# Output row stores released from one another in an attention, Fourier-mix and MLP kernel

## The chip, the cores and the metric

One core of a Trainium2 chip. The metric is device microseconds of one execution. Kernels that share a ratio were run in turn on the same chip; the experiments were timed in three calls (chips 0, 15 and 5), each with its own runs of the kernel before, so across calls compare ratios and not times. All runs quoted are in the fast state (none over 1.5% above the fastest of its kernel; two slower runs of the kernel before, at 295.54 and 295.11 us, are left out), except two single looks whose state is unknown (said where they stand). Ratios are the mean time of one kernel's runs over that of the other's of the same rounds, so not quite the ratio of the medians quoted beside them.

## The reference, cut to what matters

```python
def reference(q, k, v, sort_net, moe_w_ch1, moe_w_ch2):
    # attention over 4 batches, 8 heads, 768 tokens, head_dim 64,
    # keys and values mixed by blocks with a normalised sort_net
    x = attn_out.transpose(0, 2, 1, 3).reshape(4, 768, 512)
    mixed = real(fft(fft(x, axis=1), axis=2))
    u  = x + mixed
    un = layernorm(u)                      # no scale, no shift
    return u + maximum(un @ w_ch1, 0) @ w_ch2     # 512 -> 2048 -> 512
```

The output is 4 x 768 rows of 512 float32. The kernel computes it in 24 tiles of 128 rows: per batch a half g = 0 (tiles T = 0, 1, 2) and a half g = 1 (T = 3, 4, 5). It uses a symmetry of the Fourier transform, and the tiles of the second half therefore hold their tokens in descending order.

## The kernel before

The engines go by the profile's names: PE is TensorE (matmuls; PEld its weight loads), DVE VectorE, ACT ScalarE, POOL GpSimd, SP SyncE; a q after a name, as in POOLq, is that engine's sequencer. A store is a DMA, and it *lands* when its completion semaphore says so. A planner in the kernel records operations, puts them in an order per engine and issues them. What the change touches is the end of the MLP of one half (cuts marked):

```python
TOK = [list(range(1, 129)), list(range(129, 257)),
       list(range(257, 384)) + [0], list(range(767, 639, -1)),
       list(range(639, 511, -1)), list(range(511, 383, -1))]
# ...
many("u", 6, [128, DM], F32)            # six buffers for output tiles
# ...
for tt in range(3):
    # ... 16 matmuls of w_ch2 into bank ps ("ff2") ...
    V.tensor_tensor(u.ap, ps.ap, u.ap, op=ALU.add)          # residual add
    if T < 2:
        nc.sync.dma_start(out[b, t0:t0 + 128, :], u.ap)     # SP, plain
    elif T == 2:
        # ... three plain SP stores of 112, 15 and 1 rows ...
    else:
        i = 3 * b + T - 3
        nc.gpsimd.indirect_dma_start(                       # POOL, by row list
            out.rearrange("b s m -> (b s) m"),
            bass.IndirectOffsetOnAxis(ap=rows[:, i:i + 1], axis=0),
            u.ap, None)
```

Ascending rows go out as plain stores from SP. Descending rows go out as indirect stores from POOL, one row number per partition. The dependency tracker cannot see which rows an indirect store writes. It takes the whole output as written, and so it makes each indirect store wait for the landing of the one before, and plain and indirect stores wait for one another.

The softmax here doesn't subtract the row's maximum and nothing guards it: scores larger than these inputs give would overflow.

## Time and profile before

| | before |
|---|---|
| time, median of 4 runs | 292.62 us (291.86 to 292.87) |
| span of the profiled run (291.84 us, not one of the four) | 290.0 us |
| PE / DVE / ACT / POOL busy | 90% / 59% / 54% / 23% of the span |
| end of the last residual add | 281.57 + 0.69 = 282.26 us |
| from there to the end of the span, "the tail" | 7.74 us |

The first 110 us (loads, attention of the first batches) have idle PE; from 110 to 277 us PE is full; the tail is stores alone. The prediction shows these lines. Two more lines: what closes the span. The view is of the closing instructions of the program (count, then min/median/max in ns, first and last start in us).

```profile
L1377 SPq EVENT_SEMAPHORE  x11: 17/28/28, 288.1 to 290.0; - x11
...
L1377 POOLq DRAIN  x3: 46/97/4127, 285.1 to 289.8; - x3
```

SP gets past its wait for the last store at 288.1 us, which is its landing. POOL's closing DRAIN starts about 285.13 us, takes 4.127 us and ends at 289.26. The span ends 0.74 us later.

### The profile page before, as it was taken

How to read it: one execution, taken by the hardware profiler on the slowest of the kernel's cores; microseconds unless marked ns; L12 is line 12 of the kernel's file. 1: busy time of each engine (PE TensorE's matmuls, PEld its weight loads, DVE VectorE, ACT ScalarE, POOL GpSimd, SP SyncE). 2: the span in 40 equal slices, each digit the busy share in tenths (PEclk: the TensorE clock that was granted, in tenths of full speed). 3: DMA queues.
4: the chain of work that ended last, by engine and by line, in shares of the span. 5: the costliest groups of instructions: out<-in, count | busy, mean ns of one | idle time of the engine just before them, and what ended most of it. 6: DMA issues, size and time to landing. Idle time of an engine off the chain costs nothing.

```text
span 290.0 us, 5807 instructions
## 1 busy us (share of the span) xinstructions
PE 260.9 (90%) x2284; PEld 155.2 (54%) x2284; DVE 171.9 (59%) x405; ACT 157.9 (54%) x323; POOL 66.3 (23%) x104
## 2 busy tenths in 40 slices
PE   0389988897999999999999999999999999999980
PEld 0258866554565656554566456455555546545530
DVE  4697999999999999831579643145034226210020
ACT  2677979785778945970477037137415505425300
POOL 8973300015900640011220002032000212200021
PEclk9997999998899999999999999999999999999997
DMA  7999999910990897211113010311311111221001
GB/s 114 211 260 245 215 208 211 219 37 5 157 146 10 95 165 133 66 37 20 77 47 57 36 52 22 58 72 50 57 72 37 38 54 72 38 90 36 2 36 72
DMA packets 42529, 26.33 MB, mean 91 GB/s; under 512 B 30106, under 2 KB 38824, under 8 KB 42500
## 3 DMA queue, kind: packets, MB, share of 16 engines
q0 software_dynamic: 23536, 18.31, 37.4%
q1 hardware_dynamic: 18966, 7.64, 11.6%
q8 instruction: 18, 0.29, 0.4%
q14 instruction: 9, 0.07, 0.1%
HBM read 28.96 MB, written 6.29 MB: 122 GB/s over the span
## 4 chain that ended last, share of the span: by engine, by line
PE 62%; DVE 22%; DMA 8%; issue 3%; POOL 2%; ACT 1%; POOLq 0%; DVEq 0%
PE bank L1253 26%; PE bank L1274 25%; DMA hr<-in_v_dram 4%; DVE vsf L660 3%; DVE vcx L708 3%; DVE rt L1006 3%; DMA out_dram<-u,rows 2%; POOL kq L472 2%; DMA kq<-in_q_dram 2%; PE bank L1149 2%; PE bank L991 2%; DVE st L1186 1%; PE bank L952 1%; PE bank L897 1%; DVE ks L660 1%
## 5 line engine op out<-in xcount | busy, mean ns | idle before, releaser
L1265 ACT ACTIVATE hr<-bank 128x384 f16<-128x384 f32 x115 | 56.3, 491 | 75.2 <-PE bank L1253 74.4
L1253 PE MATMUL bank<-ut,w1sb 128*128 128x384 f16 x512 | 92.8, 329 | 0.7 <-ACT ut L660 0.7
L1274 PE MATMUL bank<-w2sb,hr 128*128 128x512 f16 x384 | 87.9, 379 | 0.0
L1253 PEld LDWEIGHTS <-w1sb 128*128 128x128 f16 x512 | 49.0, 99 | 34.8 <-issue 1.8
L1274 PEld LDWEIGHTS <-hr 128*128 128x128 f16 x384 | 36.7, 98 | 41.8 <-issue 0.2
L1282 DVE TENSOR_TENSOR u<-bank,u 128x512 f32<-128x512 f32 x24 | 16.5, 689 | 60.2 <-PE bank L1274 59.8
L961 ACT ACTIVATE ex<-bank 96x384 f32<-96x384 f32 x64 | 27.9, 485 | 6.3 <-PE bank L952 6.0
L1295 POOL DMA_INDIRECT out_dram<-u,rows x12 | 12.2, 1013 | 77.0 <-DVE u L1282 56.7
L1193 POOL TENSOR_SCALAR mv<-mv 128x3 f32<-128x3 f32 x8 | 1.9, 240 | 109.8 <-DVE mv L1188 109.8
L976 ACT ACTIVATE eb<-ex,negone 96x384 f16<-96x384 f32 x35 | 20.8, 615 | 0.2
L1213 ACT ACTIVATE un<-u,nm,ny 128x512 f16<-128x512 f32 x15 | 12.2, 810 | 11.8 <-DMA ut<-un 8.5
L1172 DVE SCALAR_TENSOR_TENSOR u<-rt,bank 128x510 f32<-128x510 f16 x12 | 8.1, 678 | 16.3 <-PE bank L1138 8.9
L991 PE MATMUL bank<-vsf,eb 97*128 97x65 f16 x416 | 16.5, 193 | 1.3 <-DVE rr L836 0.5
L1006 DVE TENSOR_TENSOR rt<-bank,rz 128x384 f16<-128x384 f32 x32 | 17.2, 549 | 0.3
L991 PEld LDWEIGHTS <-eb 97*128 97x128 f16 x416 | 15.4, 98 | 3.6 <-issue 1.3
L472 POOL DMA_DIRECT2D kq<-in_q_dram x20 | 16.4, 850 | 1.7 <-DMA kq<-in_q_dram 1.2
L1186 DVE BATCH_NORM_STATS2 st<-u 128x6 f32<-128x512 f32 x24 | 16.1, 686 | 0.3
L1160 DVE SCALAR_TENSOR_TENSOR u<-rt,bank 128x512 f32<-128x512 f16 x12 | 8.0, 684 | 13.9 <-PE bank L1153 13.5
L927 PE MATMUL bank<-pack,qr 128*128 128x128 f16 x48 | 4.8, 246 | 12.3 <-ACT qr L660 11.7
L724 PE MATMUL bank<-bdv,vcx 128*128 128x128 f16 (+1 forms) x128 | 12.6, 225 | 0.0
L952 PE MATMUL bank<-qt,ks 64*128 64x96 f16 x256 | 11.3, 207 | 1.3 <-DVE rt L1006 0.4
L897 PE MATMUL bank<-bdk,kq 128*64 128x128 f16 x192 | 10.7, 228 | 1.6 <-DVE bdk L636 0.8
(130 smaller groups left out, 338.2 us busy)
## 6 DMA issues: line engine op xcount, KB each, us to landing
kq<-in_k_dram POOLq DMA_DIRECT2D x8, 384.0 KB, 6.6
w1sb<-in_moe_w_ch_dram POOLq DMA_DIRECT2D x4, 512.0 KB, 16.0
w2sb<-in_moe_w_ch_dram POOLq DMA_DIRECT2D x4, 512.0 KB, 19.0
out_dram<-u SPq DMA_DIRECT2D x8, 256.0 KB, 2.0
kq<-in_q_dram POOLq DMA_DIRECT2D x4, 384.0 KB, 11.6
hr<-in_v_dram POOLq DMA_DIRECT2D x2, 768.0 KB, 11.2
kq<-in_v_dram POOLq DMA_DIRECT2D x2, 768.0 KB, 21.5
kq<-in_q_dram POOLq DMA_DIRECT2D x16, 96.0 KB, 5.5
```

Source lines behind the costliest of these rows:

```text
L472: o = P.add({eng: c}, lambda _: e.dma_start(dst, src), r=r, w=w, prio=prio, nbytes=nbytes, tag="load", after=after)
L897: nc.tensor.matmul(ps.ap[64 * h2:64 * h2 + 64, 128 * r3:128 * r3 + 128], k16[:, 2 * hl + h2, 3 * half + r3, :], bdk[:, 2 * hp + h2].rearra ...
L952: nc.tensor.matmul(pss[h2].ap[:, BLK * j:BLK * j + BLK], ks.ap[rows, 4 * g + j, :], qt.ap[rows, c0:c0 + BLK])
L961: nc.scalar.activation(ex.ap, pss[h2].ap[0:96, 0:384], AF.Exp, scale=SCALE),
L976: nc.scalar.activation(ed, src, AF.Identity, bias=negone[0:96])
L991: nc.tensor.matmul(po.ap[:, 65 * T:65 * T + 65], eb.ap[:, e0:e0 + 128], vsf[:, vi:vi + 65], start=(n == 0), stop=(n == len(WIN[T]) - 1), s ...
L1006: P.add({"DVE": (0.45, 0.56)}, lambda _: V.tensor_tensor(rt.ap[:, :, D * h:D * h + D], po3()[:, :, 0:D], rz.ap[:, :, None].broadcast_to([1 ...
L1186: P.add({"DVE": (0.6, 0.69)}, lambda _, u=u, st=st: V.bn_stats(st.ap, u.ap), r=[u], w=[st], tag="bn")
L1253: nc.tensor.matmul(ps.ap[:, 0:GT], w1sb[:, c, 128 * fc:128 * fc + 128], ut.ap[:, c, :], start=(c == 0), stop=(c == 3))
L1265: nc.scalar.activation(hr[g][:, fc, :], ps.ap[:, 0:GT], AF.Relu)
L1274: nc.tensor.matmul(ps.ap, hr[g][:, fc, 128 * tt:128 * tt + 128], w2sb[:, fc, :], start=(fc == 0), stop=(fc == 15))
L1282: V.tensor_tensor(u.ap, ps.ap, u.ap, op=ALU.add),
```

## The change

Each output row is stored exactly once, so no store has to wait for another. The change declares that to the dependency tracker. It puts a one-column memset ahead of each indirect store: without it the tracker refuses the release for two DMAs that are neighbours in one engine's issue order.

```diff
+    between = ct("between", [128, 1], F32)
...
                 else:
                     i = 3 * b + T - 3
-                    nc.gpsimd.indirect_dma_start(
+                    nc.gpsimd.memset(between, 0.0)
+                    st_ = [nc.gpsimd.indirect_dma_start(
                         ...
-                                                  axis=0), u.ap, None)
+                                                  axis=0), u.ap, None)]
+                for x in st_:
+                    for y in stores if T < 3 else stores + direct:
+                        tc.declare_no_dep(x.ins, y.ins,
+                                          reason="each row stored once")
+                (stores if T > 2 else direct).extend(st_)
```

(The plain stores are put in a list `st_` likewise; `stores` holds the indirect ones so far, `direct` the plain ones.)

More of the change, by code (lines that the diff above doesn't have):

```diff
@@ L1286, in f @@
                 if T < 2:
-                    nc.sync.dma_start(out[b, t0:t0 + 128, :], u.ap)
+                    st_ = [nc.sync.dma_start(out[b, t0:t0 + 128, :], u.ap)]
                 elif T == 2:
-                    nc.sync.dma_start(out[b, t0:t0 + 112, :], u.ap[0:112])
-                    nc.sync.dma_start(out[b, t0 + 112:t0 + 127, :],
-                                      u.ap[112:127])
-                    nc.sync.dma_start(out[b, 0:1, :], u.ap[127:128])
+                    st_ = [nc.sync.dma_start(out[b, t0:t0 + 112, :],
+                                             u.ap[0:112]),
+                           nc.sync.dma_start(out[b, t0 + 112:t0 + 127, :],
+                                             u.ap[112:127]),
+                           nc.sync.dma_start(out[b, 0:1, :], u.ap[127:128])]
                 else:
                     i = 3 * b + T - 3
-                    nc.gpsimd.indirect_dma_start(
+                    nc.gpsimd.memset(between, 0.0)
+                    st_ = [nc.gpsimd.indirect_dma_start(
                         out.rearrange("b s m -> (b s) m"),
                         bass.IndirectOffsetOnAxis(ap=rows[:, i:i + 1],
-                                                  axis=0), u.ap, None)
+                                                  axis=0), u.ap, None)]
[4 more added lines that the diff above has]
+                (stores if T > 2 else direct).extend(st_)
             P.add({"SP": (0.1, 2.3)} if g == 0 else {"POOL": (1.2, 3.5)}, f,
@@ L1310, in attn @@
             av(b, h)
-    goal = []
+    goal, stores, direct = [], [], []
     def at(p, *fns):
```

## The prediction

Where it calls a stretch of the trace a "second" ("the second from 287 to 288"), read microsecond.

> **What bounds the kernel now.** I read three things in this order: where TensorE has gaps (busy time by stretch), what ends the run (the chain of waits, last 31 us), and which waits concern output stores (the waits of each engine). Then I compared the two programs' instruction orders.
>
> First the stretches. Columns: stretch, length, then busy us and number of instructions for PE, PEld, DVE, ACT and POOL, the granted clock, the DMA share and GB/s.
>
> ```profile
> 110.00:145.00 35.00, 35.00 (x295) 19.30 (x292) 19.99 (x49) 19.21 (x43) 4.67 (x7) 1.00 0.27 66
> 145.00:152.00 7.00, 6.89 (x94) 4.68 (x93) 5.14 (x15) 4.88 (x11) 1.64 (x4) 1.00 0.15 50
> 152.00:200.00 48.00, 48.00 (x330) 26.38 (x328) 25.64 (x59) 20.07 (x44) 4.58 (x7) 1.00 0.19 52
> 200.00:250.00 50.00, 50.00 (x282) 27.33 (x280) 17.45 (x38) 22.21 (x45) 7.79 (x15) 1.00 0.18 49
> 250.00:277.00 27.00, 26.99 (x143) 13.69 (x141) 2.21 (x4) 9.38 (x19) 0.00 (x0) 1.00 0.19 45
> 277.00:290.00 13.00, 4.47 (x21) 1.85 (x19) 2.08 (x3) 0.00 (x0) 3.01 (x3) 0.84 0.16 61
> ```
>
> From 110 to 277 us, where all but the last stores fall, PE is busy 35.00 + 6.89 + 48.00 + 50.00 + 26.99 = 166.88 of 167 us. It loses 0.12 us. After 277 us the picture is different: 4.47 busy of 13 us. PE bounds the middle, something else bounds the end. What that is stands in the chain of waits (start, length, what):
>
> ```profile
> 263.31 7.80 PE bank L1253 x48
> 271.11 6.06 PE bank L1274 x28
> 277.17 0.03 DVEq L1282
> 277.20 0.04 issue
> 277.24 0.70 DVE u L1282
> 277.94 0.28 issue
> 278.22 2.87 DMA out_dram<-u,rows
> 281.10 0.02 issue
> 281.12 0.02 POOLq L1295
> 281.14 0.73 issue
> 281.86 2.73 DMA out_dram<-u,rows
> 284.59 0.02 issue
> 284.61 0.02 POOLq L1295
> 284.63 0.50 issue
> 285.13 1.18 POOLq L1377
> ```
>
> Busy PE can hide a slow PE, so look at the first two lines: 7.80 / 48 = 0.1625 us a 384-column matmul, 6.06 / 28 = 0.216 us a 512-column one. A piece at 176.50 us has the same pace (4.55 us for 28, 0.1625). So the middle is full in earnest. Then the chain leaves PE at 277.17 and walks from one indirect store of 128 rows to the next. Each store is released by the landing of the one before: that is the serial tail. The timeline of the tail says when the data for each was ready:
>
> ```profile
> 277.24 0.69 DVE L1282 TENSOR_TENSOR u<-bank,u 128x512 f32<-128x512 f32 x1 [13.14 <-PE bank L1274]
> 278.12 0.69 DVE L1282 TENSOR_TENSOR u<-bank,u 128x512 f32<-128x512 f32 x1 [0.19 <-PE bank L1274]
> 278.22 1.09 POOL L1295 DMA_INDIRECT out_dram<-u,rows  x1 [29.14 <-DVE u L1282]
> 281.57 0.69 DVE L1282 TENSOR_TENSOR u<-bank,u 128x512 f32<-128x512 f32 x1 [2.76 <-PE bank L1274]
> 281.86 0.97 POOL L1295 DMA_INDIRECT out_dram<-u,rows  x1 [2.55 <-DMA out_dram<-u,rows]
> 285.36 0.96 POOL L1295 DMA_INDIRECT out_dram<-u,rows  x1 [2.52 <-DMA out_dram<-u,rows]
> ```
>
> The three residual adds end at 277.93, 278.81 and 282.26; the three stores start at 278.22, 281.86 and 285.36. Store 2 stands 3.05 us after its data, store 3 stands 3.10 us after its data, store 1 only 0.28 us.
>
> **What the Trainium skill says.** (1) "DMA: Bandwidth & Descriptors", section "Two DMAs through the same engine are not ordered": only the completion semaphore orders two DMAs. So a store that must follow another has to sit out the whole landing, as it does here (2.87 and 2.73 us). These stores write different rows, so no order is needed. (2) "SBUF — State Buffer", section "The DMA setup-cost knee": a transfer takes about 2 us plus bytes / 436 GB/s. A store of 128 x 512 f32 is 262144 bytes; an estimate from that page is 2 + 0.60 = 2.60 us. The trace has 2.73 to 2.87, close; I use the trace. (3) "Perfetto Trace Analysis", section "DMA Instruction — SWDGE (GPSIMD)": the recorded end of such an instruction is the end of descriptor generation, not of the movement. The trace agrees: store 3 ends its 0.96 us at 286.32, while the second from 287 to 288 still moves 209 GB/s. So POOL is free for the next store 1 us after a store starts; the other 1.8 us need nobody.
>
> **The change part by part.** Compared engine by engine with line numbers removed, the PE, ACT and DVE programs are identical, waits included. Only two engines change.
>
> SP: three stores of the first half (one per batch from the second on) lose their waits for indirect stores of the batch before. Those had landed long ago (for the SP stores from 165 us on, the last indirect store before them started at 143.42 us). Worth 0.
>
> POOL: 12 one-column memsets come in, one ahead of each indirect store; store 2 and 3 of each group lose the wait for the one before, store 1 loses waits for SP stores which had landed. The last group's store 3 keeps one DMA semaphore (an old transfer, eight back) and DVE's.
>
> Cost of the memsets: the nearest row is a 128x1 memset at 0.20 us (one other row has 0.10). 12 x 0.20 = 2.4 us on an engine that is 23% busy. In the tail: memset 1 can run right after the normalisation at 249 us. Store 1 starts at 278.22 and holds POOL 1.09 to 279.31; memset 2 to 279.5; store 2, whose data is there since 278.81, runs about 279.5 to 280.6; memset 3 to 280.8. POOL then waits for the add that ends at 282.26. No memset is on the path.
>
> Store 3: start = 282.26 + 0.28 (the gap of store 1 after its add) = 282.54, in place of 285.36. That is 2.82 us earlier. One thing is put back. The first store after other POOL work took 1.09 us to generate and 2.87 to land, those after a store 0.97 and 2.73. With a memset ahead of each, I charge store 3 the longer figure: 0.14 us. Net: 2.82 - 0.14 = 2.68, about 2.7 us. From the start of store 3 to the end of the span is 290.0 - 285.36 = 4.64 us, of which 2.73 is landing and 1.9 the closing waits and drain; I leave the latter as it is. New span: 282.54 + 4.64 + 0.14 = 287.3.
>
> The middle: each of the three earlier groups has its stores 2 and 3 delayed by up to 2.5 us too, and DVE waits for their buffers:
>
> ```profile
> DVE u L1172 <- DMA out_dram<-u,rows: 5.5, 5, 1.7
> ```
>
> 5.5 us over five waits go. But DVE's later work feeds a PE that loses 0.12 us in all, so at most 0.12 us comes back. I count 0. It would be an error to add the 5.5 us, or the 10.1 + 10.1 us for which POOL sat idle before stores.
>
> Sum in time: 292.82 - 2.7 - 0 = 290.1 us, 0.9%.
>
> **The rivals.** (a) Nothing comes out: the drain at the end is set by something else. For it: the chain's last piece is POOL's own closing drain, which lasts 4.13 us from 285.1, longer than the landing at 288.1. Against it: SP, too, sits until a store lands, and PE, ACT and DVE are long done. Were the drain a fixed cost beside the store, it would still start after store 3 is issued, so it would move with it. It would leave 292.8 only if generation of the third store were held for another reason. I give this 5%. (b) Half a gain: stores 2 and 3 in flight together slow one another. Speaks against: store 2 would move its bytes around 281 to 282, within about 1.3 us as store 1 did (the seconds 279 to 281 at 57 and 205 GB/s), and store 3 not before 283.8. Would leave 291 to 291.5. (c) More than the tail: earlier buffers let DVE run ahead, and PE gains. Capped at 0.12 us by the gaps: 290.0. Only if PE's record hides stalls could it be 2 to 3 us more; the constant 0.1625 us a matmul speaks against it. (d) The memsets cost: if each took as long as the worst small memset (0.76 us) there would still be 282.26 - 280.6 = 1.7 us of room in the tail. If the change of POOL instruction delays the store by more than the 0.14 us, the gain shrinks: at half a us each, 290.5.
>
> **Range and chances.** Centre 290.1. Runs of before spread 0.46 us, so half of that either way; the drain and the memset switch I put at half a us up, the PE gaps and a shorter issue at half a us down. Range 289.2 to 291.1. Two per cent is 5.9 us, over twice the whole tail wait: faster 3%. Slower by 5.9 us would need a new wait that the order of instructions doesn't have: 2%. Within 2%: 95%.
>
> **What would show it.** Right: store 3 starts about 0.3 us after the third add and no longer after a landing; store 2 starts about 1.3 us after store 1; the chain of waits runs over PE to the third add and then one landing instead of two; PE's last matmul still ends near 281.5 us; DVE's 5.5 us on stores fall towards 0 without PE moving. Wrong: store 3 still waits 2 us or more after its add (then POOL was held by something other than the semaphore), the last matmul ends earlier by more than 0.3 us (then the middle mattered), or the time from store 3 to the end grows beyond 5 us (then the drain, not the landing, sets the end).

## The result, and the profile after

| | before | after |
|---|---|---|
| time, median of 4 runs | 292.62 us | 289.62 us (288.59 to 289.94) |
| ratio, 95% interval | | 0.9896 (0.9863 to 0.9928) |
| span of the profiled run | 290.0 us | 288.2 us |
| tail after the last residual add | 7.74 us | 288.2 - (282.49 + 0.69) = 5.02 us |

The result is correct. The interval lies clear of 1. The tail of the changed kernel, from its timeline (start, length, engine, line, operation, and in brackets the idle time before it and what ended that):

```profile
279.14 1.09 POOL L1298 DMA_INDIRECT out_dram<-u,rows  x1 [29.26 <-DVE u L1283]
280.24 0.12 POOL L1297 MEMSET between<- 128x1 f32 x1
280.54 0.97 POOL L1298 DMA_INDIRECT out_dram<-u,rows  x1 [0.18 <-issue]
281.50 0.11 POOL L1297 MEMSET between<- 128x1 f32 x1
282.49 0.69 DVE L1283 TENSOR_TENSOR u<-bank,u 128x512 f32<-128x512 f32 x1 [2.76 <-PE bank L1275]
283.46 0.96 POOL L1298 DMA_INDIRECT out_dram<-u,rows  x1 [1.85 <-DVE u L1283]
```

Store 2 follows store 1 by 1.40 us where it was 3.64. Store 3 starts 0.28 us after its add has ended (283.18 to 283.46) where it was 3.10. None of them waits for the landing of another any more. Busy time by stretch, with columns as in the prediction:

```profile
250.00:277.00 27.00, 27.00 (x144) 13.97 (x143) 2.97 (x5) 10.30 (x20) 0.00 (x0) 1.00 0.18 45
277.00:288.20 11.20, 5.39 (x25) 2.25 (x23) 2.07 (x3) 0.00 (x0) 3.24 (x5) 0.84 0.18 70
```

PE is as full as before up to 277 us, and its last work even ends 0.92 us later in absolute time. This profiled run was slower in its first 110 us: the residual add that stands near 109 us starts at 109.78 against 108.69. That is why the spans differ by 1.8 us and the tails by 2.7. The waits of DVE and POOL on stores changed as foreseen (total us, times, longest):

```profile
DVE u L1173 <- PE bank L1154: 7.0, 3, 2.3
```

```profile
POOL out_dram L1298 <- DVE u L1283: 67.3, 8, 29.3
```

DVE's 5.5 us of waits for indirect stores are gone; where it waits there now, it waits for PE (0.3 us for a plain store is left elsewhere). POOL's stores wait for DVE's data.

One view misleads. The chain of waits of the changed kernel does not go over PE at its end but along POOL's own order:

```profile
249.89 29.01 issue
...
283.23 1.19 POOLq L1385
```

It calls 29 us "issue" in which POOL in fact waited for data of DVE, as the timeline's brackets say. With the stores' waits gone, the view has no semaphore of a landing to follow back. A reader who went by its shares would think that instruction issue had become the bound.

The closing lines of the changed kernel, in the same view as before:

```profile
L1385 SPq EVENT_SEMAPHORE  x11: 17/28/28, 286.2 to 288.1; - x11
...
L1385 POOLq DRAIN  x3: 46/97/4140, 283.2 to 287.9; - x3
```

The last store lands at 286.2, 2.74 us after its start, as before. POOL's DRAIN takes 4.140 us from about 283.23 and ends at 287.37.

### The profile page after: what moved, and what is told of

It reads as the page before. It is cut to its first block, busy times and chain, and to the rows that moved or that the text cites. A ratio compares the mean times of both kernels' runs of the same rounds, so it can differ in the third digit from the quotient of the medians.

```text
span 288.2 us, 5805 instructions
## 1 busy us (share of the span) xinstructions
PE 261.6 (91%) x2284; PEld 155.7 (54%) x2284; DVE 171.5 (60%) x405; ACT 158.2 (55%) x323; POOL 67.7 (23%) x116
## 4 chain that ended last, share of the span: by engine, by line
PE 49%; DVE 24%; issue 16%; DMA 6%; POOL 4%; POOLq 0%; ACT 0%; DVEq 0%
PE bank L1275 19%; PE bank L1254 18%; DMA hr<-in_v_dram 4%; DVE vcx L709 3%; DVE vsf L661 3%; DVE rt L1007 2%; PE bank L992 2%; PE bank L1150 2%; PE bank L898 2%; DMA out_dram<-u 2%; DVE st L1187 1%; PE bank L953 1%; DVE eb L975 1%; DVE ks L661 1%; POOL out_dram L1298 1%
## 5 line engine op out<-in xcount | busy, mean ns | idle before, releaser
L1254 PE MATMUL bank<-ut,w1sb 128*128 128x384 f16 x512 | 91.5, 326 | 0.7 <-ACT ut L661 0.7
L661 DVE CAST vsf<-bank 96x512 f16<-96x512 f32 x16 | 11.5, 778 | 1.2 <-PE bank L728 1.1
```

Source lines behind the costliest of these rows:

```text
L661: (nc.scalar.copy if e == "ACT" else V.tensor_copy)(dst, src)
L1254: nc.tensor.matmul(ps.ap[:, 0:GT], w1sb[:, c, 128 * fc:128 * fc + 128], ut.ap[:, c, :], start=(c == 0), stop=(c == 3))
```

## The experiments

Theory A: the whole gain is the serial chain of the last group's stores; earlier groups' releases are worth nothing because PE is full. Rival B: earlier buffers also help. Rival C: the memsets cost something. Rival D: POOL's closing drain, not the landing, sets the end.

Two lengths were read in each trace, because the first 110 us vary from run to run: the **tail** (end of the last residual add to the end of the span, which is given to 0.1 us) and the **middle** (start of the residual add near 109 us to the start of the last one). The times come from several chips; compare the ratios.

| kernel | tail, us | middle, us | time, us | ratio to before (95%) |
|---|---|---|---|---|
| before | 7.74 | 172.88 | 292.62 | |
| after | 5.02 | 172.71 | 289.62 | 0.9896 (0.9863 to 0.9928) |
| after, again | 4.99 | 172.73 | 290.01 | 0.9905 (0.9854 to 0.9956) |
| only last group released | 4.94 | 172.90 | 290.99 | 0.9947 (0.9912 to 0.9982) |
| all but last group released | 7.73 | 172.72 | 292.79 | 1.0017 (0.9979 to 1.0054) |
| memsets only | 7.74 | 172.88 | 292.71 | 1.0025 (0.9990 to 1.0059) |
| last group's second store not released | 6.01 | 172.72 | 291.33 | 0.9967 (0.9938 to 0.9997) |
| 4 matmuls and a plain store last | 4.71 | 172.64 | 289.09 | 0.9896 (0.9838 to 0.9954) |
| 8 matmuls and a plain store last | 3.30 | 172.65 | 287.34 | 0.9851 (0.9820 to 0.9883) |
| 12 matmuls and a plain store last | 3.28 | 172.65 | 288.12 | 0.9868 (0.9827 to 0.9909) |

**Only the last group released**

```diff
-                for x in st_:
+                for x in st_ if b == B - 1 and T > 2 else []:
```

> Only the three indirect stores of the last group are released from other stores; all earlier stores wait as before. Measure: the tail, from the end of the last residual add to the end of the span (7.74 us before, 5.02 us in the changed kernel). Theory (the gain is the last group's serial chain alone): tail 5.0 us, ratio to before about 0.990 as for the full change, DVE's waits for indirect stores stay near 5.5 us. Rival (the earlier buffers help too): tail 5.0 us, but the time is 0.3 us or more above the full change, and PE's idle time between 110 us and its last matmul is larger than the full change's.

The tail fell to 4.94 us, as in the full change, and DVE's waits for indirect stores stayed at 5.5 us. So the tail is the last group's affair. The middle stayed at 172.90, against 172.71 and 172.73 in two traces of the full change. The time missed its expectation: ratio 0.9947 with 0.990 outside its interval, and 1.4 us above the full change by the medians, which was to be a sign of the rival. The two profiled runs, 1.3 us apart in span, show where it lies: 1.19 us before the add near 109 us, which this run reached only at 110.97, and 0.19 us in the middle.

**All but the last group released**

```diff
-                for x in st_:
+                for x in st_ if not (b == B - 1 and T > 2) else []:
```

> The opposite part: all stores released except the three indirect stores of the last group. Theory (the middle is worth nothing since PE is full there): tail 7.7 us, ratio 1.000 within the noise (291.9 to 293), although DVE's 5.5 us of waits for indirect stores fall to about 0. Rival (earlier buffers let PE run ahead): 0.3 us or more faster than before, tail still 7.7 us, last matmul earlier against the start of the steady middle.

The tail is back at 7.73 us, with stores 2 and 3 released by landings as before:

```profile
282.86 0.96 POOL L1298 DMA_INDIRECT out_dram<-u,rows  x1 [2.43 <-DMA out_dram<-u,rows]
...
286.36 0.96 POOL L1298 DMA_INDIRECT out_dram<-u,rows  x1 [2.42 <-DMA out_dram<-u,rows]
```

No gain can be seen in the times (1.0017). But the middle is 172.72, as short as in the full change, and DVE's waits for indirect stores are gone. So rival B holds in small: the earlier releases are worth 172.88 - 172.72 = 0.16 us. All of it falls between two adds: 239.66 to 256.43 before (16.77 us), 240.83 to 257.43 here (16.60 us). The same stretch takes 16.76 to 16.77 us in the three traces without the earlier releases and 16.60 us in all nine with them. The timeline there, of the kernel before and of the changed one:

```profile
244.81 5.36 PE L1253 MATMUL bank<-ut,w1sb 128*128 128x384 f16 x32
...
245.34 0.69 DVE L1172 SCALAR_TENSOR_TENSOR u<-rt,bank 128x510 f32<-128x510 f16 x1 [1.66 <-DMA out_dram<-u,rows]
...
250.19 7.28 PE L1274 MATMUL bank<-w2sb,hr 128*128 128x512 f16 x33
```

```profile
245.91 5.36 PE L1254 MATMUL bank<-ut,w1sb 128*128 128x384 f16 x32
...
246.10 0.69 DVE L1173 SCALAR_TENSOR_TENSOR u<-rt,bank 128x510 f32<-128x510 f16 x1 [2.34 <-PE bank L1154]
...
251.10 7.29 PE L1275 MATMUL bank<-w2sb,hr 128*128 128x512 f16 x33
```

Before, DVE builds a tile 0.53 us after PE's block begins, held by a store's landing; afterwards 0.19 us after it. PE's next block begins 5.38 us after this one began, against 5.19. Yet PE counts as busy throughout, and the block is 5.36 us long in both. In between stand the tile's statistics, its scale from POOL, its normalisation on DVE and, next in DVE's order, a ReLU that PE's next block waits for. That ReLU before and after:

```profile
249.59 0.55 DVE L1262 TENSOR_SCALAR hr<-bank 128x384 f16<-128x384 f32 x1
```

```profile
250.35 0.55 DVE L1263 TENSOR_SCALAR hr<-bank 128x384 f16<-128x384 f32 x1
```

In the packed traces the first matmul of the next block carries a wait for DVE, by the built program for this ReLU. Before, it starts at 250.19 us, 0.05 us after the ReLU ends and 0.33 us after the matmul ahead of it; afterwards it starts 0.2 us after the ReLU's end and 0.16 us after the matmul ahead of it, the usual pace. So PE lost 0.17 us to this ReLU. That the late tile made the ReLU late I read from DVE's order; no run isolates it. The Trainium skill warns of this in "Trainium Kernel Development and Optimization", section "Performance Expectations": matmul busy time is a bad measure of how close a kernel is to its roofline, because matmuls are pipelined. Here one matmul is recorded as 0.33 us long while the next starts 0.16 us after it, and so the loss left no gap.

**Memsets only**

```diff
-                for x in st_:
-                    for y in stores if T < 3 else stores + direct:
-                        tc.declare_no_dep(...)
```

> The twelve memsets come in, but no store is released. Theory (memsets run while POOL waits for a landing, so they are hidden): tail 7.7 us, ratio 1.000. Rival (memset plus change of instruction is on the chain, 0.12 us busy and up to 0.2 us of issue before each of stores 2 and 3): tail 8.0 to 8.4 us, ratio 1.001 to 1.002.

Tail 7.74, middle 172.88, both as before to 0.01 us; ratio 1.0025, not clear of 1. A memset takes 0.12 us and runs while POOL waits for the landing; in the changed kernel's trace the first one stands at 125.88 us, so the first 110 us can't pay for it. Rival C falls.

**The last group's second store not released**

```diff
-                for x in st_:
+                for x in st_ if not (b == B - 1 and T == 4) else []:
```

> In the last group the first and third store are released as in the change, the second still waits for the landing of the first. Theory (one in-order POOL queue: the third store starts once its own data is there and the second has generated its descriptors and the memset is done): second store 3.6 us after the first, third 1.25 to 1.3 us after the second, that is about 0.85 us after the third add ends in place of 0.28; tail 5.6 us, about 0.6 us slower than the full change. Rival (the third store's own wait is all that counts): third store 0.28 us after its add, tail 5.0 us.

The tail is 6.01 us: the in-order queue holds, the rival falls, but 0.4 us more than expected. The stores 2 and 3:

```profile
283.51 0.97 POOL L1298 DMA_INDIRECT out_dram<-u,rows  x1 [2.85 <-DVE u L1283]
...
284.78 0.96 POOL L1298 DMA_INDIRECT out_dram<-u,rows  x1 [0.19 <-issue]
```

Store 3 is free and its data are there since 283.49, yet it starts at 284.78, 1.27 us after store 2, because POOL issues in order. Store 2 itself came 4.06 us after store 1 (279.45), not 3.64. My edit had a side effect. In the built program the one store that is not released from anything names 17 semaphores, since none of the earlier stores is known to have landed by way of another. POOL's sequencer walks through them:

```profile
L1298 POOLq EVENT_SEMAPHORE  x8: 42/43/2971, 279.2 to 282.7; - x8
```

The third of them holds for 2.97 us, until the landing of store 1 (about 282.4); five more, 42 to 43 ns each, follow, the last starting at 282.7. The store begins about 0.75 us after that last one, the distance that it has in the kernel before (281.12 to 281.86). The bracket's "DVE" is a coincidence of times: store 2's own data had been there since 280.03. So a partial release has a price of its own: the waits that remain may be spelled out one by one.

**The changed kernel again**

No edit; the full change.

> The changed kernel unaltered, timed again on the chip of this call, beside the two below and in more rounds. Theory (tail 2.7 us shorter, middle 0.17 us shorter): ratio 0.990, tail 5.0 us, from the residual add near 109 us to the last one 172.7 us as against 172.9 us before. If the earlier gap between the full change and the release of the last group alone (1.5 us by the medians) was noise of the first 100 us, the ratio comes out nearer 0.992 than 0.988.

Ratio 0.9905, tail 4.99, middle 172.73: both parts of the gain repeat. The question stays open: 0.9905 is neither clearly nearer 0.992 nor 0.988. The six runs went from 288.73 to 292.21, so times alone can't settle a fraction of a microsecond here.

**What closes the run: a short last store (wrong result)**

```diff
-                                                  axis=0), u.ap, None)]
+                                                  axis=0), u.ap, None)] if i < 11 else [
...
+                            bass.IndirectOffsetOnAxis(ap=rows[0:16, i:i + 1],
+                                                      axis=0), u.ap[0:16], None)]
```

> Wrong result on purpose: the last indirect store of all writes 16 of its 128 rows. Asks what closes the run: POOL's closing drain of 4.13 us or the landing. Theory landing: fewer rows, shorter descriptor generation and landing (2.0 to 2.3 us in place of 2.74), the drain shrinks by the same, tail 4.3 to 4.6 us. Rival (the drain is a fixed 4.13 us after the last indirect store is issued): the drain stays at 4.1 us and the tail at 5.0 us.

The store landed at 285.9, 2.23 us after its start at 283.67 in place of 2.74. The drain shrank by the same:

```profile
L1389 POOLq DRAIN  x3: 46/97/3629, 283.4 to 287.6; - x3
```

It is 3.629 us where it was 4.140: 0.51 less, as is the landing. The store's own POOL time fell by only 0.09 us (0.96 to 0.87), so the drain does not follow that. Tail 287.8 - 283.39 = 4.41 us. So the drain is not fixed. In the packed traces it ends 1.18 us after SP gets past its wait for the last indirect store, to 0.01 us in eleven of the twelve (in the plain-store look below SP is still issuing its own store at that moment). As a fixed cost, rival D falls; but the drain is what stands between the landing and the end.

**The last tile by a plain store (wrong rows)**

```diff
+                elif (b == B - 1 and T == 5):
+                    st_ = [nc.sync.dma_start(out[b, t0 - 127:t0 + 1, :], u.ap)]
```

A plain store of descending rows (a negative row step) does not compile, so this one writes the right number of rows in the wrong order. It asks only for time.

> Wrong result on purpose: the last tile goes out by a plain SP store, its rows in ascending order where they belong in descending. Order of work unchanged. Theory (the indirect form costs 0.25 us more to start and 0.7 us more to land): SP store starts 0.05 us after the third add, lands 2.0 us later, closing 1.9 us: tail 3.95 us, POOL's drain ends earlier than that and does not count. Rival (the closing after the landing is longer for this queue, or the drain is a fixed cost that still counts): tail 4.5 us or more.

Tail 285.1 - 281.93 = 3.17 us, 0.8 less than expected. The SP store starts 0.02 us after its add (281.95) and SP gets past it at 284.0, 2.0 us later. The closing after the landing is 1.1 us, not 1.9: POOL's drain ended earlier, with its own last landing. So the 1.9 us that I had taken as fixed belong to an indirect store as the last one: 1.18 us of drain and about 0.75 us of barrier (the instructions by which the engines wait for one another at the end).

**A correct version with a plain store last: 4 matmuls moved**

The last quarter of the w_ch2 matmuls of one tile of the last batch's first half (T = 1, ascending rows) is held back behind all other matmuls, in a bank of its own:

```diff
+            if (b, g, tt) == (B - 1, 0, 1):
+                ps = Buf("pf")
+                tile_(tt, ps, (0, 1, 2))
+                held.append(lambda: tile_(1, ps, (3,), tuple(ff2s[-12:])))
...
+    held[0]()
```

> The changed kernel with four matmuls (the last quarter of one tile of the last batch's first half, kept in a bank of its own) moved behind all others, so that the last store is a plain SP store, and the three indirect stores are 0.86 us earlier against the last add. The result stays correct. Theory (the end is set by the last landing plus the closing, whichever queue): SP store starts about 0.05 us after the last add and lands 2.0 us later; the last indirect store's end, 0.28 + 4.64 us after an add 0.86 us before the last, gives 4.06 us: tail 4.0 to 4.1 us, 0.9 to 1.0 us faster than the changed kernel, ratio to before about 0.987. Rival (the four late matmuls or the missing bank cost PE something): tail 4.1 us, but the middle from the add near 109 us to the last grows by 0.3 us or more and the gain is eaten.

Correct, but the tail is 4.71 us, 0.65 more than expected: a miss. The two last stores:

```profile
282.48 0.95 POOL L1301 DMA_INDIRECT out_dram<-u,rows  x1 [1.85 <-DVE u L1286]
283.02 0.35 SPq L1291 DMA_DIRECT2D out_dram<-u  x1
```

They start 0.54 us apart. The indirect store took 3.3 us to land in place of 2.74, at 285.8; from 284 to 285 us the DMA engines moved 401 GB/s, against 262 at most in the tail of the changed kernel. Both stores were in flight at once and shared the engines, as the skill says of DMAs from different issuing engines ("DMA: Bandwidth & Descriptors", section "Issuing engines are not separate DMA queues"). Then came POOL's drain on the delayed landing, 4.692 us long. The middle is 172.64 us, so the four late matmuls cost PE nothing.

**8 and 12 matmuls moved**

```diff
-                tile_(tt, ps, (0, 1, 2))
-                held.append(lambda: tile_(1, ps, (3,), ...))
+                tile_(tt, ps, (0, 1))
+                held.append(lambda: tile_(1, ps, (2, 3), ...))
```

and with `(0,)` and `(1, 2, 3)` for twelve.

> As the kernel with four matmuls moved to the end, but eight: the three indirect stores now come 1.7 us ahead of the last add, so that the last indirect store moves its bytes before the SP store moves its own. What the earlier kernel showed: two stores in flight together (both landed about 0.6 to 0.75 us late), and POOL's closing drain ends about 1.15 us after the last indirect landing, after which 0.75 us of barrier follow. Theory (overlap and drain were what ate the gain): indirect store lands 1.0 us + 0.3 us after the last add, its drain and barrier end 3.2 us after it; SP store lands 2.05 us after the add and closes 1.1 us later: tail 3.2 to 3.5 us, 1.5 to 1.8 us faster than the changed kernel, ratio about 0.985. Rival (an SP store at the end always lands late here, 2.8 us): tail 4.0 us or more.

> Twelve matmuls moved to the end, 2.6 us between the last indirect data and the last add. Theory: the indirect stores are out of the way altogether: SP landing 2.0 us after the add, tail 3.2 us. Only 36 in place of 40 matmuls now stand before the first that needs the transposed tile: if its landing was less than 0.86 us ahead, the middle grows by the rest, up to 0.5 us. Rival (drain or overlap still matter): tail above 3.5 us.

Eight: tail 285.3 - 282.00 = 3.30 us; twelve: 286.6 - 283.32 = 3.28 us. Both as expected; the middle is 172.65 in both, so PE lost nothing and the fear for twelve fell. With eight, the indirect store (280.62) and the plain one (282.03) start 1.4 us apart, which is enough. The version with eight has the lowest ratio to the kernel before, 0.9851. Against the changed kernel its tail is 1.7 us shorter in the traces; their times were taken in different rounds and their intervals overlap a little, so a gain in time over the changed kernel is not shown directly.

## Why the prediction was right

Predicted 290.1 us, range 289.2 to 291.1; measured 289.62. By its own steps:

- **What bounds the kernel.** Right. The gain is in the tail, 7.74 to 5.02 us. Releasing only the last group gives all of that, releasing all the others none of it.
- **Store 3 starts 0.28 us after its add, 2.82 us earlier.** Right to the hundredth: 3.10 to 0.28 us.
- **0.14 us charged to store 3 for the change of POOL instruction.** Not seen: it generated for 0.96 us and landed 2.74 us after its start, as before. The tail fell by 2.72 us with spans rounded to 0.1 us; the packed traces hold them as 290.041 and 288.154 us, and with these it fell by 2.81, while the time from store 3 to the end is 4.69 us in both. So the 2.82 stood whole, and the 0.14 taken off was wrong.
- **Memsets off the path.** Right: 0.12 us each where I had 0.20, tail and middle unchanged by them alone. Rival (d) has a wrong sum: its 1.7 us of room is counted with memsets of 0.20 us. With 0.76 us each the third would end near 282.0, with 0.3 us of room. Its conclusion is the same.
- **The middle counts 0, at most 0.12 us.** Mis-sized. It gave 0.16 to 0.17 us. The cap was taken from PE's idle time, and a loss of 0.17 us between two matmuls leaves no idle time in PE's record, as shown above. Rival (c) had named this chance, at 2 to 3 us. My guard, the constant pace of 0.1625 us a matmul, looked inside blocks; the stall lay between two of them. The warning not to add DVE's 5.5 us was right: they brought 3% of that.
- **Rival (a), the drain.** It is not a fixed cost that keeps the gain away, but it is not neutral either: it follows the last indirect landing by 1.18 us. I had put it into a fixed 1.9 us. That did no harm here and cost me an expectation in the plain-store look.
- **Rival (b), stores in flight together.** Not in the changed kernel: the bytes of store 2 moved before 283 us, those of store 3 after 284.9. It is real when stores come closer, as the version with four matmuls showed.
- **The signs to look for.** Store 3 came 0.28 us after its add, store 2 1.40 us after store 1 (about 1.3 expected), and DVE's 5.5 us fell away. The chain of waits did not run over PE; it went along POOL's order and called the time "issue". PE's last matmul ended near 282.4 us, not 281.5, because of the slower start, and PE did gain the 0.17 us of the middle. None of the signs of being wrong came.

Tail and middle together are 2.81 + 0.17 = 2.98 us, where 2.7 was predicted; the two misses, 0.14 us put back and 0.17 us not counted, went the same way. The ratio says 292.62 x (1 - 0.9896) = 3.04 us, with an interval of 2.1 to 4.0, too wide to tell 2.7 from 3.0: it is the traces that decide, and that the time came within 0.5 us of the prediction is partly luck. What spreads the times is the first 110 us, which took from 108.4 to 111.0 us in the twelve traces. The four traces that were through them by 109.1 us had a mean granted clock (the share of TensorE's full speed that was allowed) of 0.96 from 20 to 60 us, the other eight 0.83 to 0.91. But the one at 0.83 was through at 109.66, ahead of all that had 0.91; that the clock is the cause is not shown.

## What to carry to other kernels

Where the last stores of a kernel wait for one another, look at the last group first: here it gave all of the tail's gain. Its worth was the start of the last store less the time at which its own data were ready, less the 0.28 us that a store takes to start in any case: read it from the timeline before touching anything. Don't add up the waits in the middle; but if an engine counts as full, compare the distance between fixed instructions in two traces rather than its busy time. Then ask which store should come last: a plain one, with the slow-to-close indirect ones far enough ahead not to overlap it, shortened the tail by another 1.7 us here.

## What the Trainium skill lacked or had wrong

- "VectorE: DVE Perf Modes", section "The DRAIN you can't avoid", names two kinds of DRAIN: the flush after each VectorE instruction and the runtime's own, a constant of about 12 ns on all engines. The DRAIN with which the kernel's own program closes is neither, and no page that I found has it: on POOL it is 3.6 to 4.9 us here and ends 1.18 us after the landing of the last indirect store; about 0.75 us of barrier follow. A plain store last closes in 1.1 us, an indirect one in 1.9.
- "SBUF — State Buffer", section "The DMA setup-cost knee": its formula gives 2.60 us for 256 KB. Measured 2.0 us for the plain SP store and 2.73 to 2.87 us for the indirect POOL store of the same size; one formula does not fit both. (The section says itself that the fit overstates at mid sizes; it does not tell the two kinds of store apart.)
- "DMA: Bandwidth & Descriptors", section "Issuing engines are not separate DMA queues", is right that stores share the engines, but has no number for what that costs a landing: two 256 KB stores started 0.54 us apart made the first land in 3.3 us in place of 2.74.
- No page that I found says what a long list of waits on one POOL store costs: 42 to 43 ns for each sequencer instruction once satisfied, and a store that starts about 0.75 us after the last such instruction once one of them has waited for a landing, against 0.28 us after the end of a DVE instruction.
